# The first product of a Winograd-style MLP kernel: partial results copied into PSUM banks that later products accumulate onto

## The chip, the cores and the metric

The kernel runs on one core of one Trainium2 chip. The metric is the device time of one launch in microseconds (us); the time quoted is the median of the runs shown. Everything below refers to one profiled execution of the kernel before, with a span of 764.3 us from its first to its last instruction.

## The reference

Block-diagonal softmax attention over chunks of 64 tokens, then a gated two-layer MLP, all in fp32:

```python
scores = scale * np.matmul(q_c, k_c.transpose(0, 1, 2, 4, 3))   # 8 x 8 heads, chunks of 64, head_dim 64
attn = softmax(scores)                                          # over each chunk's 64 keys
x = np.matmul(attn, v_c)                                        # as x: (4608 tokens, 512)
h = x @ w_in                                                    # 512 -> 2048
g = h * np.clip(h + 3.0, 0.0, 6.0) / 6.0
return g @ w_out                                                # 2048 -> 512
```

## The kernel before, in words

The 4608 tokens are 9 blocks of 512. Block 0 takes the MLP in the plain way. The other eight are four pairs, 0 to 3; for each pair both matrix products are cut two by two and done with seven half-size products instead of eight (the Strassen-Winograd scheme). Every fp32 operand is split into a high and a low part, so that each 128x128x512 product is three matmuls (`passes`, L473 high by high, L474 high by low, L475 low by high); L475 alone reads the weights' low part.

**The early stage** (the first 100 us or so) loads the weights, and for each half-weight tile ScalarE makes two pieces, VectorE joins them (L215), ScalarE or VectorE takes the high part (L223, L221), and VectorE the low part (L226). For block 0 TensorE alternates the steps `a`, `b` of a tile (first product into an `h` bank, 12 matmuls in all) and `c` (12 matmuls of the second product, onto the four `acc` banks). A tile's gate is ScalarE's relu (L495), VectorE's product (L498, which frees the `h` bank), then high (L502, ScalarE) and low part (L505, VectorE). There are two `h` banks, so tile 3's `a` needs tile 1's L498 done. Between these stand the steps of the next block's attention: scores (L263), then on VectorE maximum (L275), subtraction (L279), sum (L286), reciprocal and scaling (L309) and a transposition (L335), on ScalarE the swaps that complete it (L345, five copies), on TensorE the product with v (L367).

**A pair's first product** (`first_product`, L1040) goes over 8 feature pairs p (pair 0 over 4 of them; 28 periods in all). One period is seven products of six matmuls each, named by their Winograd number in the order `ORDER_A`, and a combination on VectorE:

```python
ORDER_A = (1, 5, 6, 7, 2, 3, 4)
# p1 = copy of 1 (ScalarE, L1090); u2 = 6 + p1; u4 = 5 + u2; s7 = 7 + u4; s3 = 3 + u4; s4 = 4 + u2 (VectorE, L1032)
```

Product 2 is accumulated onto bank 1, and 3 and 4 onto the banks of 5 and 7, once these have been read. So TensorE waits, within a period, for p1 ahead of 2, for u4 ahead of 3, for s7 ahead of 4. Each of the four results then has a relu (L907, ScalarE) and a gate product (L910, VectorE). Partial banks come from two rings, `h` (two banks, also used by the attention's products) and `acc` (four).

**The order of the work** on every engine is fixed before the program runs: `Schedule.order` (L102) is a list scheduler that takes each step's named predecessors, its cost and its due time, and writes one list per engine. A due time is passed back along the chain of predecessors, so changing one step's successors can move instructions anywhere in the program, on engines that the edit does not touch. On the chip every engine takes its list strictly in order.

Of the kernel before, what the change touches and what calls it, by code (L numbers as in the profile page):

```python
# [9 lines left out]
F32 = mybir.dt.float32  # L10
# [8 lines left out]
P = 128  # L19
# [14 lines left out]
PLAIN = [p + q + NFP * r for p in range(0, NPL, 2) for r in range(2) for q in range(2)]  # L34
FIRST = {0: list(range(NFT)), 1: PLAIN, 2: PLAIN}
HELD = {5: 0, 6: 4, 7: 1, 4: 5}
ORDER_A = (1, 5, 6, 7, 2, 3, 4)
ORDER_B = (1, 5, 6, 7, 2, 4, 3)
SLOTS = 7 * NFP
HALF = [slice(0, CH), slice(CH, P)]  # L40
# [109 lines left out]
def tile_kernel(ctx: ExitStack, tc: tile.TileContext, qk_in, v_in, weights, out):  # L150
# [85 lines left out]
    class Attention:  # L236
# [116 lines left out]
        def product(self, bank=None, part=(0, 1)):  # L353
            if part[0]:
                po = self.po
            elif bank:
                po = [bank().rearrange("p (a i t) -> p a i t", a=2, t=CH) for _ in HALF]
                self.src = [t.rearrange("p a i t -> p (a i) t") for t in po]
            else:
                t = self.out()  # L360
                po = self.po = [t[:, s].rearrange("p (a i t) -> p a i t", a=2, t=CH) for s in range(2)]
                self.src = t.rearrange("p s (k t) -> p s k t", t=CH)
            for a in part:
                for i in range(NB // 2):
                    for s, rows in enumerate(HALF):
                        for o in HALF:
                            PE.matmul(po[s][o, a, i, :], lhsT=self.v[rows, a, i, o], rhs=self.aT[rows, a, i, o], start=True, stop=True)  # L367

        def parts(self, x):

# [640 lines left out]
    SLOT_OF = (2, 0, 5, 6, 4, 1, 3, 7)  # L1011
    FREED = (3, 5, 7, 2, 6, 4, 1, 0)

    bank = lambda i: ps_h.tile([P, NT], F32, name="h") if i in (6, 3) else ps_o.tile([P, NT], F32, name="acc")
    take_bank = lambda i, name, until: work.take("h", 2, name, until) if i in (6, 3) else work.take("o", 4, name, until)
    fetches, shared = 0, None

    def add_fetch(s, after=()):
# [21 lines left out]
    def first_product(s):  # L1040
        work.add(f"lay{s}", "none", 0.0, [f"ul{s - 1}.{i}.{k}" for i in ORDER_B for k in range(NFP // 2)] if s else [f"out{et}" for et in range(NET)], lambda: None)
        before = f"s{s - 1}.{SLOTS - 1}" if s else f"b{2 * NFT + PLAIN[-1]}"
        g = GRAIN[s]
        ceil = lambda n: (n + g - 1) // g
        laid = {}
        for at, p in enumerate(turns(s) if s else range(NPL, NFP), 0 if s else NPL):
            t = {}
            more = lambda r, p=p: left(p + NFP * r) if s == 0 else [f"less{u}s" for u in LATER] if s == 1 and p < 2 else [f"send{u}" for u in LATER] if s == 1 and p < NPL else []
            gq = lambda r, c, p=p: gate_of(r, c, p)
            id_ = lambda name, p=p: f"{name}{s}.{p}"  # L1050
            feeds = [add_fetch(s, [f"own{NFP + p}", f"send{NFP + p}"] if s == 1 else []) for _ in range(ceil(4) + ceil(3))] if s else []
            for k, i in enumerate(ORDER_A):
                name = id_(f"f{i}.")
                j = {2: 1, 3: 5, 4: 7}.get(i, i)
                feed, until = feeds[ceil(4) * (k // 4) + k % 4 // g] if s else (None if i in (1, 2, 4) else f"less{NFP + p}s", [])
                over = s and (k % 4 % g == g - 1 or k == 6)
                after = [before, feed, f"x{s}.{i}l" if s or i in HELD else None]
                if i == j:
                    after += take_bank(i, name, [id_({1: "gate2.", 5: "gate3.", 7: "gate4.", 6: "gate7."}[i])])
                else:  # L1060
                    after.append(id_({2: "p1.", 3: "u4.", 4: "s7."}[i]))

                def product(i=i, j=j, k=k, t=t, over=over, p=p):
                    w = ahead[0][:, k % 4 % g] if s else weight_of(p, i)
                    ps = t[j] if i != j else keep_tile(t, i, lambda: bank(i))
                    for ct in range(2):
                        o = slice(ct * P, ct * P + P)
                        passes(ps, w[:, 0, o], w[:, 1, o], *operand(s, i, ct), i == j and ct == 0, ct == 1, i != j)
                    if over:
                        ahead.pop(0)  # L1070

                due = START[s] + PART * (7 * at + k)
                work.add(name, "PE", PART, after, product, due=due)
                before = name
                if over:
                    until.append(name)
                of = lambda j, t=t: lambda: t[j]

                def fresh(key, p=p):
                    if s:  # L1080
                        return (up if key == "u2" else tp).tile([P, NT], F32, name=key)
                    if p % 2 == 0:
                        laid[key] = pair_of(("p1", "u2", "u4").index(key), F32)
                    return laid[key][:, p % 2]

                new = lambda key, t=t, fresh=fresh: lambda: keep_tile(t, key, lambda: fresh(key))
                ring = "" if s else "first"
                if i == 1:
                    work.add(id_("p1."), "ACT", 0.59, [name, f"lay{s}", *work.take(ring + "p1", 2, id_("p1."), [id_("u2.")])],
                             lambda o=new("p1"), x=of(1): ACT.copy(out=o(), in_=x()), due=due)  # L1090
                elif i == 6:
                    work.add(id_("u2."), "DVE", 0.69, [name, id_("p1."), *work.take(ring + "u2", 3 if s else 2, id_("u2."), [id_("s3."), id_("s4.")])],
                             add(new("u2"), of(6), of("p1")), due=due)
                    work.add(id_("u4."), "DVE", 0.69, [id_("f5."), id_("u2."), *work.take(ring + "u4", 2, id_("u4."), [id_("s7.")])],
                             add(new("u4"), of(5), of("u2")), due=due)
                elif i == 7:
                    work.add(id_("s7."), "DVE", 0.69, [name, id_("u4.")], add(of(6), of(7), of("u4")), due=due)
                    add_relu_gate(id_("7."), id_("s7."), of(6), lambda f=gq: f(1, 1), due, more(1))
                elif i == 2:
                    add_relu_gate(id_("2."), name, of(1), lambda f=gq: f(0, 0), due, more(0))  # L1100
                elif i in (3, 4):
                    out = (lambda f=gq: f(0, 1)) if i == 3 else (lambda f=gq: f(1, 0))
                    work.add(id_(f"s{i}."), "DVE", 0.69, [name, id_("u2.")], add(of(j), of(j), of("u2")), due=due)
                    add_relu_gate(id_(f"{i}."), id_(f"s{i}."), of(j), out, due, more(int(i == 4)))
                    if i == 3 and s:
                        on = (DVE, "DVE", 0.69) if (s, p) in TDVE else (POOL, "POOL", 1.45)
                        work.add(id_("t1."), *on[1:], [id_("gate3."), id_("gate2.")], lambda f=gq, on=on[0]: on.tensor_tensor(  # L1107
                            out=f(0, 1), in0=f(0, 1), in1=f(0, 0), op=ALU.subtract))
                        work.add(id_("t2."), *on[1:], [id_("t1."), id_("gate7.")], lambda f=gq, p=p, on=on[0]: on.tensor_tensor(
                            out=t2_of(p), in0=f(1, 1), in1=f(0, 1), op=ALU.add))  # L1110
            place_at(("f", s, at), bank_h)

    def add_units(s):
# [5 lines left out]
        if s == 0:  # L1119
            for p in range(NFP):  # L1120
                gates = [f"gate{2 * NFT + p}", f"gate{NFT + p}"] if p < NPL else [f"gate3.0.{p}", f"gate2.0.{p}"]
                work.add(f"t1.0.{p}", *(("POOL", 1.45) if TPOOL else ("DVE", 0.69)), gates, lambda p=p: (POOL if TPOOL else DVE).tensor_tensor(
                    out=gate_of(0, 1, p), in0=gate_of(0, 1, p), in1=gate_of(0, 0, p), op=ALU.subtract))
                free = {0: [f"out{et}" for et in range(NET)], 1: [f"u2.0.{NFP - 1}"], 2: [f"s7.0.{NFP - 1}"], 3: [f"s3.0.{NFP - 1}", f"s4.0.{NFP - 1}"]}[p // 2]
# [172 lines left out]
```

## Time and profile before

| | |
|---|---|
| median of 3 runs | 765.55 us (765.48 to 766.66) |
| span of the profiled execution, and its instructions | 764.3 us, 13998 |
| TensorE matmul / VectorE / ScalarE / GpSimd busy | 757.2 / 640.9 / 451.2 / 69.9 us |
| share of the span | 99% / 84% / 59% / 9% |
| granted TensorE clock | 1.000 over the whole span |

The profile gives the profiled execution by its span alone; the median of the runs is 1.25 us above that, which is taken as what lies around the span. TensorE's matmuls are recorded with modelled ends, so its busy share says only that it is never long without work; waits are read from the distance between the starts of successive matmuls.

### The profile page before, as it was taken

The numbers are of one execution on the slowest core, as the hardware profiler recorded it, in microseconds if no ns is written. First come the engines' busy times: TensorE is split into PE (matmuls) and PEld (weight loads), VectorE is DVE, ScalarE is ACT, GpSimd is POOL, SyncE is SP. The second block draws the span as 40 slices with busy tenths as digits, with TensorE's granted clock in tenths as the row PEclk, the third lists the DMA queues.
The fourth block names the chain that finished last, engine by engine and source line by source line (L and its number), as shares of the span: only waits on it lengthen the run. The fifth ranks groups of instructions, "written<-read, shape, count | busy, mean of one in ns | idle before, by whom it ended". The sixth has DMA issues, their size and how long they took to land.

```text
span 764.3 us, 13998 instructions
## 1 busy us (share of the span) xinstructions
PE 757.2 (99%) x5457; PEld 621.4 (81%) x5457; DVE 640.9 (84%) x805; ACT 451.2 (59%) x884; POOL 69.9 (9%) x74
## 2 busy tenths in 40 slices
PE   8999999999999999999999999999999999999998
PEld 5788788888888888788888888888888888888887
DVE  6989989898999999898999697689996667679751
ACT  6898967675768844356884444557853333355330
POOL 0000000000000010121200103201001123221010
PEclk9999999999999999999999999999999999999999
DMA  9999999959486898986667865757657666565572
GB/s 370 406 361 374 330 354 343 314 206 313 168 288 242 294 389 279 319 267 211 216 241 243 315 229 195 256 195 274 197 195 238 218 211 193 194 207 193 193 242 90
DMA packets 67442, 198.05 MB, mean 259 GB/s; under 512 B 7024, under 2 KB 19568, under 8 KB 63024
## 3 DMA queue, kind: packets, MB, share of 16 engines
q1 hardware_dynamic: 64752, 188.90, 71.9%
q0 software_dynamic: 2480, 8.13, 2.7%
q8 instruction: 43, 0.70, 0.4%
q14 instruction: 23, 0.19, 0.1%
q10 hardware_dynamic: 144, 0.13, 0.1%
HBM read 153.09 MB, written 44.04 MB: 258 GB/s over the span
## 4 chain that ended last, share of the span: by engine, by line
PE 85%; DMA 5%; DVE 5%; ACT 3%; issue 1%; SPq 0%; DVEq 0%; ACTq 0%
PE acc L473 21%; PE acc L474 20%; PE acc L475 20%; PE h L473 7%; PE h L474 7%; PE h L475 7%; DMA wb<-w_in_out 3%; PE two L263 2%; PE h L367 1%; DMA wb<-wa 1%; DMA xd<-qk_in 1%; ACT r L212 1%; ACT e L345 1%; ACT u L208 1%; DVE u L215 1%
## 5 line engine op out<-in xcount | busy, mean ns | idle before, releaser
L473 PE MATMUL acc<-wa,ws 128*128 128x512 f32 (+1 forms) x536 | 208.8, 390 | 0.5 <-DVE u L1032 0.5
L474 PE MATMUL acc<-wa,ws 128*128 128x512 f32 (+1 forms) x536 | 207.8, 388 | 0.0
L475 PE MATMUL acc<-wa,ws 128*128 128x512 f32 (+1 forms) x536 | 207.8, 388 | 0.0
L1140 ACT CAST wa<-wb 128x1024 fp32r<-128x1024 f32 x96 | 100.1, 1053 | 78.2 <-PE acc L475 49.1
L1144 DVE TENSOR_TENSOR wa<-wb,wa 128x1024 fp32r<-128x1024 f32 x96 | 119.0, 1257 | 17.3 <-ACT wa L1140 17.2
L473 PEld LDWEIGHTS acc<-wa,ws 128*128 128x128 f32 x536 | 100.6, 188 | 22.2 <-DVE u L1032 1.3
L475 PEld LDWEIGHTS acc<-wa,ws 128*128 128x128 f32 x536 | 100.6, 188 | 20.7
L474 PEld LDWEIGHTS acc<-wa,ws 128*128 128x128 f32 x536 | 100.7, 188 | 20.2
L907 ACT ACTIVATE r<-acc,half 128x512 f32<-128x512 f32 x90 | 61.8, 688 | 35.6 <-DVE acc L1032 31.2
L907 ACT ACTIVATE r<-h,half 128x512 f32<-128x512 f32 x38 | 26.3, 692 | 86.1 <-DVE h L1032 81.4
L910 DVE SCALAR_TENSOR_TENSOR wb<-r,acc 128x512 f32<-128x512 f32 x90 | 61.1, 681 | 6.1 <-ACT r L907 6.0
L474 PE MATMUL h<-wa,ws 128*128 128x512 f32 (+1 forms) x144 | 55.2, 383 | 0.0
L475 PE MATMUL h<-wa,ws 128*128 128x512 f32 (+1 forms) x144 | 55.2, 383 | 0.0
L473 PE MATMUL h<-wa,ws 128*128 128x512 f32 (+1 forms) x144 | 55.2, 383 | 0.0
L298 ACT ACTIVATE e<-two,m 128x64 f32<-128x64 f32 x160 | 48.4, 333 | 7.8 <-DVE m L292 6.4
L1172 POOL DMA_DIRECT2D out_t<-o x15 | 8.4, 557 | 429.6 <-DVE o L1165 428.5
L1107 POOL TENSOR_TENSOR wb<-wb 128x512 f32<-128x512 f32 x18 | 25.1, 1396 | 174.7 <-DVE wb L910 142.9
L1032 DVE TENSOR_TENSOR u<-h,p 128x512 f32<-128x512 f32 x32 | 21.9, 687 | 22.8 <-PE h L475 21.9
L1032 DVE TENSOR_TENSOR acc<-acc,u 128x512 f32<-128x512 f32 x48 | 33.0, 694 | 5.8 <-PE acc L475 5.8
L298 ACT ACTIVATION_READ_ACCUMULATOR e<-two,m 128x1 f32 x160 | 36.1, 225 | 0.0
L910 DVE SCALAR_TENSOR_TENSOR wb<-r,h 128x512 f32<-128x512 f32 x38 | 25.8, 680 | 10.7 <-ACT r L907 10.7
L473 PE MATMUL acc<-wa,wa 128*128 128x512 f32 x88 | 34.6, 393 | 0.0
(247 smaller groups left out, 1460.5 us busy)
## 6 DMA issues: line engine op xcount, KB each, us to landing
ws<-b SPq DMA_DIRECT2D x84, 512.0 KB, 4.6
ws<-a SPq DMA_DIRECT2D x72, 512.0 KB, 4.6
qk<-qk_in SPq DMA_DIRECT2D x17, 1024.0 KB, 7.6
wa<-b SPq DMA_DIRECT2D x28, 512.0 KB, 5.8
v<-v_in SPq DMA_DIRECT2D x17, 512.0 KB, 5.3
wa<-w_in_out SPq DMA_DIRECT2D x8, 1024.0 KB, 12.0
wb<-w_in_out SPq DMA_DIRECT2D x8, 1024.0 KB, 11.1
a<-wa SPq DMA_DIRECT2D x32, 256.0 KB, 4.8
```

Source lines behind the costliest of these rows:

```text
L263: PE.matmul(self.s[to, a, 2 * i + k, :], lhsT=self.qk[rows, 0, 2 * i + s, o], rhs=self.qk[rows, 1, 2 * i + s, o], start=True, stop=True)
L298: ACT.activation(out=self.flat(self.e)[:, c], in_=self.flat(self.s)[:, c], func=AF.Exp, bias=self.m[:, c:c + 1], scale=SCALE, accum_out=se ...
L473: PE.matmul(ps, lhsT=a_h, rhs=b_h, start=first, stop=False, skip_group_check=more)
L474: PE.matmul(ps, lhsT=a_h, rhs=b_l, start=False, stop=False, skip_group_check=more)
L475: PE.matmul(ps, lhsT=a_l, rhs=b_h, start=False, stop=last, skip_group_check=more)
L907: ACT.activation(out=t["r"], in_=ps(), func=AF.Relu, bias=half, scale=1.0 / 6.0)
L910: work.add("gate" + name, "DVE", 0.69, ["relu" + name, *more], lambda: DVE.scalar_tensor_tensor(out=out(), in0=t["r"], scalar=1.0, in1=ps( ...
L1032: return lambda: DVE.tensor_tensor(out=out(), in0=x(), in1=y(), op=ALU.add)
L1107: work.add(id_("t1."), *on[1:], [id_("gate3."), id_("gate2.")], lambda f=gq, on=on[0]: on.tensor_tensor(out=f(0, 1), in0=f(0, 1), in1=f(0, ...
L1140: ACT.copy(out=g_ops[s, i, pp][:, :, 0], in_=src())
L1144: work.add(low, *(("POOL", 2.5) if on else ("DVE", 1.22)), [high], lambda i=i, pp=pp, src=src, on=POOL if on else DVE: on.tensor_tensor(ou ...
L1172: nc.gpsimd.dma_start(out=out[out_rows, out_cols], in_=sums_at[out_rows.start, out_cols.start])
```

## The change

In the pairs' first product three ScalarE copies take the place of three VectorE sums. Product 1's bank is copied into the bank in which product 6 will accumulate (6 then holds u2 by itself); that bank is copied into product 7's bank (7 then holds u2 + 7, and later 4 is accumulated on it); product 5 is copied to SBUF (p5) and added to 7 and to 3 on VectorE. Product 3 accumulates on 6's bank. The order becomes 1, 5, 6, 2, 7, 3, 4. Product 1 comes from the `h` ring, 5, 6 and 7 from the `acc` ring, in the second product 1, 6 and 2 from `h`. In the attention's product into separate banks only the first four matmuls start a bank. TensorE now waits for p1 ahead of 6 and of 2, for u2 ahead of 7 and of 3, for s7 ahead of 4.

```diff
-ORDER_A = (1, 5, 6, 7, 2, 3, 4)
+ORDER_A = (1, 5, 6, 2, 7, 3, 4)
...
-                            PE.matmul(po[s][o, a, i, :], lhsT=self.v[rows, a, i, o], rhs=self.aT[rows, a, i, o], start=True, stop=True)
+                            PE.matmul(po[s][o, a, i, :], lhsT=self.v[rows, a, i, o], rhs=self.aT[rows, a, i, o], start=not bank or a == i == 0, stop=True, skip_group_check=bool(bank))
...
-    bank = lambda i: ps_h.tile([P, NT], F32, name="h") if i in (6, 3) else ps_o.tile([P, NT], F32, name="acc")
+    bank = lambda i: bank_h() if i in (1, 6, 2) else bank_o()
...
+                after = [before, feed, f"x{s}.{i}l" if s or i in HELD else None, f"lay{s}" if i == 1 else id_({5: "lie.", 6: "p1.", 2: "p1.", 7: "u2.", 3: "u2.", 4: "s7."}[i])]
+                if i == 1:
+                    after += work.take("h", 2, name, [id_("gate2.")])
+                    work.add(id_("lie."), "none", 0.0, [f"lay{s}", *[x for last in ("gate7.", "gate3.") for x in work.take("o", 4, id_("lie."), [id_(last)])]],
+                             lambda t=t: t.update({j: bank_o() for j in (5, 6)}), due=due)
...
+                        passes(t[{2: 1, 3: 6, 4: 7}.get(i, i)], w[:, 0, o], w[:, 1, o], *operand(s, i, ct), fresh and ct == 0, ct == 1, not fresh)
...
                 if i == 1:
-                    work.add(id_("p1."), "ACT", 0.59, [name, f"lay{s}", *work.take(ring + "p1", 2, id_("p1."), [id_("u2.")])],
-                             lambda o=new("p1"), x=of(1): ACT.copy(out=o(), in_=x()), due=due)
+                    work.add(id_("p1."), "ACT", 0.59, [name, id_("lie.")], copy(6, 1), due=due)
+                elif i == 5:
+                    work.add(id_("p5."), "ACT", 0.59, [name, *work.take("p1" if s else "first", 2, id_("p5."), [id_("s7."), id_("s3.")])], copy("p5", 5, beside), due=due)
                 elif i == 6:
-                    work.add(id_("u2."), "DVE", 0.69, [name, id_("p1."), *work.take(ring + "u2", 3 if s else 2, id_("u2."), [id_("s3."), id_("s4.")])],
-                             add(new("u2"), of(6), of("p1")), due=due)
-                    work.add(id_("u4."), "DVE", 0.69, [id_("f5."), id_("u2."), *work.take(ring + "u4", 2, id_("u4."), [id_("s7.")])],
-                             add(new("u4"), of(5), of("u2")), due=due)
+                    work.add(id_("u2."), "ACT", 0.59, [name, *work.take("o", 4, id_("u2."), [id_("gate4.")])], copy(7, 6, bank_o), due=due)
                 elif i == 7:
-                    work.add(id_("s7."), "DVE", 0.69, [name, id_("u4.")], add(of(6), of(7), of("u4")), due=due)
+                    work.add(id_("s7."), "DVE", 0.69, [name, id_("p5.")], plus(5, 7), due=due)
...
+                elif i == 4:
+                    add_relu_gate(id_("4."), name, of(7), lambda f=gq: f(1, 0), due, more(1))
+                else:
+                    work.add(id_("s3."), "DVE", 0.69, [name, id_("p5.")], plus(6, 6), due=due)
```

The scheduler's lists move in the early stage too, well ahead of the first pair. VectorE, before, from the low part of the second half-weight tile of `w_in` (`wa1`) on; `two` is the next block's attention, `wb0` the first tile of `w_out`, `g2` the gate of tile 0, `r_510` that of tile 1:

```order
L226 TENSOR_TENSOR wa1_475<-u_418,wa1_475 128x2x512
L215 SCALAR_TENSOR_TENSOR u_479<-u_479,r_487 128x1024
L505 TENSOR_TENSOR g2_505<-r_471,g2_505 128x512
L498 SCALAR_TENSOR_TENSOR r_510<-r_510,h_447 128x512
L226 TENSOR_TENSOR wb0_519<-u_479,wb0_519 128x2x512
L215 SCALAR_TENSOR_TENSOR u_462<-u_462,r_522 128x1024
L505 TENSOR_TENSOR g0_533<-r_510,g0_533 128x512
L275 TENSOR_REDUCE m_560<-two_332 128x16
```

VectorE, now, from the same instruction on (`r_511` is tile 1's gate):

```order
L226 TENSOR_TENSOR wa1_475<-u_418,wa1_475 128x2x512
L275 TENSOR_REDUCE m_498<-two_332 128x16
L215 SCALAR_TENSOR_TENSOR u_479<-u_479,r_487 128x1024
L505 TENSOR_TENSOR g2_507<-r_471,g2_507 128x512
L279 TENSOR_TENSOR two_332<-two_332,m_498 128x1024
L226 TENSOR_TENSOR wb0_523<-u_479,wb0_523 128x2x512
L498 SCALAR_TENSOR_TENSOR r_511<-r_511,h_447 128x512
```

The attention's maximum and subtraction stand ahead of the low part of `wb0` now, and tile 1's gate product behind it. TensorE at the same place, now (`h_500` is tile 2's first product, `acc` the second product of tile 0, which before came after half of tile 3's first product):

```order
L474 MATMUL h_500<-xd_442,wa1_475 128x512
L475 MATMUL h_500<-xd_442,wa1_475 128x512
L473 MATMUL acc_539<-g2_507,wb0_523 128x512
L474 MATMUL acc_539<-g2_507,wb0_523 128x512
L475 MATMUL acc_539<-g2_507,wb0_523 128x512
L473 MATMUL acc_546<-g2_507,wb0_523 128x512
```

Tile 0's second product is six matmuls earlier in TensorE's list than before. ScalarE in pair 0's first period, now (L1087 are the copies: `acc<-h` p1, `g1<-acc` p5, `acc<-acc` u2; L345 the swaps of an attention block):

```order
L1087 COPY acc_1969<-h_1972 128x512
L1087 COPY g1_2005<-acc_1968 128x512
L345 COPY two_1698<-e_1834 128x512
L345 COPY e_1834<-e_1834 32x16x32 x2
L1087 COPY acc_2019<-acc_1969 128x512
L907 ACTIVATE r_2022<-h_1972,half_93 128x512
```

Three of the five swap copies stand between p5 and u2 here; in pair 3 the list of a period is p1, p5, u2 and the four relus, with nothing between the three copies but in its last period.

## Rows read from the trace of the kernel before

**Rows 1.** The page's first part: busy time, share of the span, instructions.

```profile
PE 757.2 (99%) x5457; PEld 621.4 (81%) x5457; DVE 640.9 (84%) x805; ACT 451.2 (59%) x884; POOL 69.9 (9%) x74
```

**Rows 2.** TensorE's own waits by releaser: us in total, times, longest.

```profile
PE acc L473 <- DVE u L1032: 0.5, 1, 0.5
...
PE two L367 <- ACT e L345: 0.3, 1, 0.3
...
PE acc L473 <- DVE g L1032: 0.2, 1, 0.2
```

**Rows 3.** Timeline of TensorE at two waits: start, duration (us), instruction, [idle before, releaser].

```profile
180.18 0.39 PE L475 MATMUL acc<-xc,wa 128*128 128x512 f32 x1
180.73 0.50 PE L473 MATMUL acc<-xd,hl 128*128 128x512 f32 x1 [0.16 <-DVE g L1032]
181.07 0.40 PE L474 MATMUL acc<-xd,hl 128*128 128x512 f32 x1
...
320.87 0.39 PE L475 MATMUL acc<-wa,ws 128*128 128x512 f32 x1
321.81 0.50 PE L473 MATMUL acc<-wa,ws 128*128 128x512 f32 x1 [0.55 <-DVE u L1032]
```

**Rows 4.** Timeline of VectorE, 24 to 38 us.

```profile
24.97 1.22 DVE L226 TENSOR_TENSOR wa<-u,wa 128x1024 fp32r<-128x1024 f32 x1
26.63 1.22 DVE L215 SCALAR_TENSOR_TENSOR u<-u,r 128x1024 int32<-128x1024 int32 x1 [0.44 <-ACT r L212]
27.77 0.68 DVE L505 TENSOR_TENSOR g<-r,g 128x512 fp32r<-128x512 f32 x1
28.37 0.68 DVE L498 SCALAR_TENSOR_TENSOR r<-r,h 128x512 f32<-128x512 f32 x1
28.97 1.23 DVE L226 TENSOR_TENSOR wb<-u,wb 128x1024 fp32r<-128x1024 f32 x1
...
31.85 1.22 DVE L275 TENSOR_REDUCE m<-two 128x16 f32<-128x1024 f32 x1
...
36.49 1.23 DVE L279 TENSOR_TENSOR two<-two,m 128x1024 f32<-128x1024 f32 x1
```

**Rows 5.** Timeline of TensorE, 25 to 34 us.

```profile
25.80 0.46 PE L263 MATMUL two<-qk 64*64 64x64 f32 x16
...
28.82 0.39 PE L475 MATMUL h<-xd,wa 128*128 128x512 f32 x1
29.11 0.50 PE L473 MATMUL h<-xa,wa 128*128 128x512 f32 x1
...
30.60 0.40 PE L473 MATMUL acc<-g,wb 128*128 128x512 f32 x1
...
33.34 0.39 PE L473 MATMUL h<-xd,wa 128*128 128x512 f32 x1
```

**Rows 6.** Timeline of ScalarE, 27 to 34 us.

```profile
27.89 1.06 ACT L223 CAST wb<-u 128x1024 fp32r<-128x1024 f32 x1 [0.19 <-DVE u L215]
...
33.15 1.14 ACT L212 ACTIVATE r<-wb 128x1024 int32<-128x1024 uint32 x1 [0.73 <-DMA wb<-w_in_out]
```

**Rows 7.** Groups of instructions by line: relu, sum onto a bank, copy p1.

```profile
L907 ACT ACTIVATE r<-acc,half 128x512 f32<-128x512 f32 x90 | 61.8, 688 | 35.6 <-DVE acc L1032 31.2 <-PE acc L475 3.5 <-DVE wb L910 0.6
...
L1032 DVE TENSOR_TENSOR acc<-acc,u 128x512 f32<-128x512 f32 x48 | 33.0, 694 | 5.8 <-PE acc L475 5.8
...
L1090 ACT COPY p<-acc 128x512 f32<-128x512 f32 x24 | 14.0, 582 | 5.8 <-PE acc L475 5.8
```

**Rows 8.** Timeline of ScalarE at an attention block's swaps.

```profile
257.66 0.59 ACT L345 COPY two<-e 128x512 f32<-128x512 f32 x1 [1.55 <-DVE e L335]
258.28 1.26 ACT L345 COPY e<-e 32x512 f32<-32x512 f32 x2
```

**Rows 9.** Timelines at pair 1's first period: product 1's last matmul, then p1 on ScalarE.

```profile
286.71 0.39 PE L475 MATMUL acc<-wa,ws 128*128 128x512 f32 x1
...
287.14 0.59 ACT L1090 COPY p<-acc 128x512 f32<-128x512 f32 x1 [0.96 <-PE acc L475]
```

More of the change, by code (lines that the diff above doesn't have):

```diff
@@ L1012, in tile_kernel @@
     FREED = (3, 5, 7, 2, 6, 4, 1, 0)
-    bank = lambda i: ps_h.tile([P, NT], F32, name="h") if i in (6, 3) else ps_o.tile([P, NT], F32, name="acc")
-    take_bank = lambda i, name, until: work.take("h", 2, name, until) if i in (6, 3) else work.take("o", 4, name, until)
+    bank = lambda i: bank_h() if i in (1, 6, 2) else bank_o()
+    take_bank = lambda i, name, until: work.take("h", 2, name, until) if i in (1, 6, 2) else work.take("o", 4, name, until)
     fetches, shared = 0, None
@@ L1053, in first_product, with product @@
                 name = id_(f"f{i}.")
-                j = {2: 1, 3: 5, 4: 7}.get(i, i)
                 feed, until = feeds[ceil(4) * (k // 4) + k % 4 // g] if s else (None if i in (1, 2, 4) else f"less{NFP + p}s", [])
                 over = s and (k % 4 % g == g - 1 or k == 6)
[L1057 to L1063, printed above, removed]
+                due = START[s] + PART * (7 * at + k)
+                after = [before, feed, f"x{s}.{i}l" if s or i in HELD else None, f"lay{s}" if i == 1 else id_({5: "lie.", 6: "p1.", 2: "p1.", 7: "u2.", 3: "u2.", 4: "s7."}[i])]
[3 more added lines that the diff above has]
+                             lambda t=t: t.update({j: bank_o() for j in (5, 6)}), due=due)
+                def product(i=i, k=k, t=t, over=over, p=p):
                     w = ahead[0][:, k % 4 % g] if s else weight_of(p, i)
-                    ps = t[j] if i != j else keep_tile(t, i, lambda: bank(i))
+                    fresh = i in (1, 5)
+                    if i == 1:
+                        t[1] = bank_h()
                     for ct in range(2):
                         o = slice(ct * P, ct * P + P)
-                        passes(ps, w[:, 0, o], w[:, 1, o], *operand(s, i, ct), i == j and ct == 0, ct == 1, i != j)
+                        passes(t[{2: 1, 3: 6, 4: 7}.get(i, i)], w[:, 0, o], w[:, 1, o], *operand(s, i, ct), fresh and ct == 0, ct == 1, not fresh)
                     if over:
                         ahead.pop(0)
-                due = START[s] + PART * (7 * at + k)
                 work.add(name, "PE", PART, after, product, due=due)
@@ L1076, in first_product @@
                     until.append(name)
-                of = lambda j, t=t: lambda: t[j]
[L1079 to L1086, printed above, removed]
@@ L1087, in first_product, with beside, copy, plus @@
-                ring = "" if s else "first"
+                def beside(p=p):
+                    if s:
+                        return tp.tile([P, NT], F32, name="p1")
+                    if p % 2 == 0:
+                        laid[0] = pair_of(1, F32)
+                    return laid[0][:, p % 2]
+                def copy(to, of, fresh=None, t=t):
+                    return lambda: ACT.copy(out=keep_tile(t, to, fresh) if fresh else t[to], in_=t[of])
+                def plus(to, of, t=t):
+                    return lambda: DVE.tensor_tensor(out=t[to], in0=t[of], in1=t["p5"], op=ALU.add)
@@ L1096, in first_product @@
                 elif i == 7:
-                    work.add(id_("s7."), "DVE", 0.69, [name, id_("u4.")], add(of(6), of(7), of("u4")), due=due)
-                    add_relu_gate(id_("7."), id_("s7."), of(6), lambda f=gq: f(1, 1), due, more(1))
+                    work.add(id_("s7."), "DVE", 0.69, [name, id_("p5.")], plus(5, 7), due=due)
+                    add_relu_gate(id_("7."), id_("s7."), of(5), lambda f=gq: f(1, 1), due, more(1))
                 elif i == 2:
                     add_relu_gate(id_("2."), name, of(1), lambda f=gq: f(0, 0), due, more(0))
[L1101 to L1104, printed above, removed]
+                elif i == 4:
+                    add_relu_gate(id_("4."), name, of(7), lambda f=gq: f(1, 0), due, more(1))
+                else:
+                    work.add(id_("s3."), "DVE", 0.69, [name, id_("p5.")], plus(6, 6), due=due)
+                    add_relu_gate(id_("3."), id_("s3."), of(6), lambda f=gq: f(0, 1), due, more(0))
@@ L1123, in add_units @@
                     out=gate_of(0, 1, p), in0=gate_of(0, 1, p), in1=gate_of(0, 0, p), op=ALU.subtract))
-                free = {0: [f"out{et}" for et in range(NET)], 1: [f"u2.0.{NFP - 1}"], 2: [f"s7.0.{NFP - 1}"], 3: [f"s3.0.{NFP - 1}", f"s4.0.{NFP - 1}"]}[p // 2]
+                free = {3: [f"s3.0.{NFP - 1}"]}.get(p // 2, [f"out{et}" for et in range(NET)])
                 work.add(f"t2.0.{p}", *(("POOL", 1.45) if TPOOL else ("DVE", 0.69)), [f"t1.0.{p}", f"gate{2 * NFT + NFP + p}" if p < NPL else f"gate7.0.{p}", *free], lambda p=p: (POOL if TPOOL else DVE).tensor_tensor(
```

## The prediction, made before the changed kernel ran

> **What bounds the kernel now.** I read the busy shares first: TensorE is busy for 757.2 of 764.3 us, VectorE for 640.9, ScalarE for 451.2 [rows 1]. That share says only that TensorE is never long idle, so next I looked for its waits, since only a wait of TensorE can be won back. After the first 20 us, which the change leaves as they are, the wait list has three [rows 2]: 0.5 and 0.2 us on a VectorE sum, both in a pair's first product, and 0.3 us on the attention's swaps at 81 us. The true price is read from starts. In full flow a matmul starts every 0.228 us: 12 of them take from 30.60 to 33.34 [rows 5]. At 180.18 the next two starts take 0.89 us in place of 0.46, so 0.43 us is lost. At 320.87 the next start takes 0.94, and the one behind a wait takes 0.34 [rows 3], so 0.82 is lost. The wait at 81 us costs 0.28 plus the same 0.11 of restart, 0.4. All that could be won is 0.43 + 0.82 + 0.4, or 1.6 us: 0.2% of the time, about what a measurement of this kernel can tell from no change (1.53 us). The 16% of idle time on VectorE and what it is freed of are worth nothing beyond these waits.
>
> **The change, part by part.** *Sums and copies.* In 28 periods VectorE loses three sums of 0.69 us each (58 us), ScalarE gains two copies of 0.58 (33 us) [rows 7]. Neither is time of TensorE. The PSUM-to-PSUM copy is not in the trace; the nearest rows are p1 out of PSUM (0.58) and the swap into PSUM (0.59) [rows 7, 8]. I take 0.58, and up to 0.8 would still be hidden below. The number of matmuls is the same, so their time is.
>
> *The old waits.* u4 no longer exists, so the waits of 0.43 and 0.82 us go: 1.25 us. What is late next is in the following item.
>
> *New waits with one product of cover.* Product 6 follows p1 with only product 5 (6 x 0.228 = 1.37 us) between, 7 follows u2 with only 2, and 4 follows s7 with only 3. p1 starts 0.43 us after the start of product 1's last matmul (286.71 to 287.14) [rows 9], ends at 1.01, and a release costs 0.06 (VectorE's gate product ends at 29.05, TensorE starts at 29.11) [rows 4, 5]. Product 6 is due at 7 x 0.228 = 1.60, so 0.5 us is spare; for s7, at 0.69 us, 0.4. What is queued ahead decides. The longest honest chain is relu 2, gate 2, s7: relu 0.43 to 1.12, gate to 1.86, s7 to 2.5, release 2.6, against product 4's due time at 13 x 0.228 = 2.96: 0.3 to 0.4 is left. So an undisturbed period costs nothing. Where ScalarE has one instruction of 0.6 to 1.1 us between two copies it still fits, as the copies are 1.37 us or more apart. I went through the 28 periods in the new lists and found one that does not fit: pair 0's first, where the swaps stand between p5 and u2. p5 starts at 0.43, the swaps take 0.59 and 1.26 [rows 8], so u2 starts near 2.8 and is through at 3.4, product 7 is due at 2.96: 0.5 us lost. For the rest I take 0.2 us in all, between 0 and 1. Behind u2 stand relu 2 and the later swaps, so they slip by as much, but the attention's product stands in front of product 4 there and covers it.
>
> *The early stage.* This is where the lists moved most, with no edit there. VectorE's list now has the attention's maximum right behind the low part of wa1. The scores end at 26.26 [rows 5], VectorE is free at 26.19 [rows 4], so the maximum starts at about 26.3. A 1024-column instruction holds VectorE for 1.14 us (26.63 to 27.77), a 512-column one for 0.60 [rows 4]. So: join 27.5, low part of tile 0's gate 28.6, subtraction 29.2, low part of wb0 30.35, and its 1.23 us end at 31.6. Before, it started at 28.97 and ended at 30.20 [rows 4]. The high part on ScalarE follows the join by 1.06 us [rows 6] and is not the late one. TensorE meets it sooner: tile 0's second product now comes right behind tile 2's first product, whose last matmul starts at 28.82 [rows 5]. Its third matmul (L475) needs the low part; it would start at 28.82 + 3 x 0.228 = 29.5, and now starts at 31.6 + 0.06. With the restart, 2.1 + 0.1 = 2.2 us. Before, tile 3 lost 0.06 waiting for its bank, and 0.11 of restart, at 29.11 [rows 5], so the net loss is 2.1 us. Tile 3's first product, which needs VectorE's gate product behind wb0 (free at 32.2), comes at 34.0 and waits for nothing.
>
> Carrying the same addition down VectorE's list, with ScalarE held at 33.15 by the load of wb1 as before [rows 6], the low part of wa2 comes at 40.0 and tile 2's gate at 42.9, each 0.3 to 0.4 us after TensorE wants it. I take 0.6 us for the two, between 0 and 1.2, since eight instructions are added up. From there TensorE is some 2.7 us later than before, and VectorE and ScalarE are not, so the wait of 0.4 us at 81 us goes.
>
> *Moved banks, queues and order.* In the second product the banks of 1, 2 and 3 change rings; a product there is 48 matmuls, 10.9 us, and each bank's last reader is a copy or sum near the start of such a stretch. I cost it at nothing; without that cover a late VectorE sum would cost about its own 0.7 us. SP's list moves a few loads and stores past one another; the loads that TensorE stood close to (wa2, wb1, wa3) keep their places. GpSimd's list keeps its kinds and order.
>
> **The sum:** 2.1 + 0.6 - 0.4 - 1.25 + 0.5 + 0.2 = +1.75 us on 764.3, say 766.1. The median shown stands 1.25 above the profiled span, so **767.3 us**. With the bounds of the early follow-ups and of the tight waits (0 to 1.2, 0 to 1) this case alone reaches from 766.2 to 768.9.
>
> **The rivals.**
>
> *The early loss is smaller and the gains hold* (the other side). Mechanism: VectorE reaches the maximum only if the scores' last piece is there; if the scheduler's list lets TensorE run on, or VectorE does the subtraction in the shadow of a later load, the low part of wb0 is late by 1 us instead of 2.1, and tiles 2 and 3 repay the rest, as VectorE has 0.44 us idle ahead of the join [rows 4]. The swap's 0.5 us goes as well if the flip comes before p5. Price: 1.0 - 1.6 = -0.6, or 764.9 us; it decides at an early loss below 1.6 us. For it: the three waits are real and do go. Against: both lists are strictly in order, and the low part is five instructions down. Should the early loss be nil, 764.0, the most that can be gained.
>
> *A repeating gap.* If something of 0.2 us that I don't see (a slower copy between banks, a late release) sits on the relu-gate-s7 chain, it is paid in every period: 28 x 0.2 = 5.6 us, 772.9. It decides where a period's spare 0.3 us is gone. For it: three waits per period have half the cover they had. Against: every link has its duration in a row. The Trainium skill speaks for this one (Perfetto Trace Analysis, Identifying the Most-Contended Engine): the same gap repeating on the engine that should be saturated can mean too little PSUM for the next tile. By it the change, which holds three accumulating banks per period instead of releasing sums to SBUF, would show such gaps. The trace before has no repeating gap, two waits in 28 periods, so I give it little.
>
> *The change does nothing that counts.* Lists and waits end where they were: 765.5.
>
> **How the numbers follow.** The forecast 0.70, of which two thirds lie over the 0.2% line (767.08): 0.47 slower, 0.23 same. The smaller early loss 0.17: 0.12 same, 0.05 faster. The repeating gap 0.10, slower. Nothing that counts 0.03, same. Faster 0.05, same 0.38, slower 0.57. The range leaves out the repeating gap and the best half of the smaller loss: from 765.2, and above to 769.8, the forecast's own upper end and one more wait of a microsecond.
>
> **What would show it.** Right: a gap of about 2 us in TensorE near 29.5, released by VectorE's L226 on wb0; tile 3's first product at about 34.0 where TensorE had finished the same work at 32; no wait of TensorE on VectorE near 320; one wait of half a microsecond on a ScalarE copy in pair 0's first period; VectorE's busy time down by 58 us and ScalarE's up by 33. Wrong: TensorE runs through 29 to 32 us; or a gap at every seventh product.

## The result, and the profile of the changed kernel

The changed kernel takes 773.97 us (median of 4 runs, 773.76 to 774.18), the kernel before in the same comparison 765.76: a ratio of 1.0107 (95% interval 1.0094 to 1.012), 8.2 us slower. The forecast was 767.3 us with a range up to 769.8: the sign was right, the size was not. Of the profiled execution (span 772.4 against 764.3) the first part of the page and TensorE's wait list (releaser, us in total, times, longest):

```profile
PE 759.8 (98%) x5457; PEld 622.3 (81%) x5457; DVE 588.6 (76%) x721; ACT 484.2 (63%) x940; POOL 70.5 (9%) x74
```

```profile
PE acc L475 <- issue: 3.7, 1, 3.7
PE acc L475 <- DVE wb L226: 1.1, 1, 1.1
...
PE acc L473 <- DVE acc L1090: 0.7, 1, 0.7
PE acc L473 <- ACT wb L223: 0.6, 1, 0.6
...
PE acc L473 <- ACT acc L1087: 0.2, 1, 0.2
```

VectorE has 52 us less to do (58 were forecast; of two sums back to back the next starts 0.60 us after the last, so that 0.09 of each 0.69 overlaps) and ScalarE 33 more [rows 1], and the wait list has grown from three entries of the pairs and the attention [rows 2] to five. Its longest has no releaser at all: "issue" means that the engine waited for nothing that the profile shows.

The early stage is the one that was forecast. VectorE, 25 to 33 us:

```profile
25.07 1.22 DVE L226 TENSOR_TENSOR wa<-u,wa 128x1024 fp32r<-128x1024 f32 x1
26.44 1.22 DVE L275 TENSOR_REDUCE m<-two 128x16 f32<-128x1024 f32 x1 [0.15 <-PE two L263]
27.59 1.22 DVE L215 SCALAR_TENSOR_TENSOR u<-u,r 128x1024 int32<-128x1024 int32 x1
...
29.32 1.23 DVE L279 TENSOR_TENSOR two<-two,m 128x1024 f32<-128x1024 f32 x1
30.45 1.22 DVE L226 TENSOR_TENSOR wb<-u,wb 128x1024 fp32r<-128x1024 f32 x1
```

and TensorE, 28 to 33 us:

```profile
28.94 0.39 PE L475 MATMUL h<-xd,wa 128*128 128x512 f32 x1
29.93 0.50 PE L473 MATMUL acc<-g,wb 128*128 128x512 f32 x1 [0.61 <-ACT wb L223]
30.27 0.40 PE L474 MATMUL acc<-g,wb 128*128 128x512 f32 x1
31.72 0.50 PE L475 MATMUL acc<-g,wb 128*128 128x512 f32 x1 [1.06 <-DVE wb L226]
```

and ScalarE's high part:

```profile
28.84 1.05 ACT L223 CAST wb<-u 128x1024 fp32r<-128x1024 f32 x1
```

The maximum and the subtraction stand ahead of the low part of `wb0`, which starts at 30.45 and not at 28.97 [rows 4]; TensorE restarts at 31.72 (forecast 31.66). The high part on ScalarE was late too (it ends at 29.89, where TensorE could have gone on at 29.17), so the loss is in two pieces.

What was not forecast is at 269 us, in pair 0's second product. TensorE there:

```profile
267.87 1.11 PE L263 MATMUL two<-qk 64*64 64x64 f32 x64
268.91 0.50 PE L473 MATMUL acc<-wa,wa 128*128 128x512 f32 x1
269.25 0.40 PE L474 MATMUL acc<-wa,wa 128*128 128x512 f32 x1
273.34 0.50 PE L475 MATMUL acc<-wa,wa 128*128 128x512 f32 x1 [3.69 <-issue]
273.68 0.48 PE L473 MATMUL acc<-wa,wa 128*128 128x512 f32 x1
273.96 0.63 PE L474 MATMUL acc<-wa,wa 128*128 128x512 f32 x1
```

and the same stretch by windows (us, busy time and count by engine, granted clock, DMA share, GB/s):

```profile
265.00:270.00 5.00, 4.65 (x139) 3.55 (x137) 5.00 (x5) 3.58 (x5) 0.66 (x2) 1.00 0.93 283
270.00:275.00 5.00, 1.66 (x5) 1.33 (x6) 2.09 (x4) 0.00 (x0) 0.00 (x0) 0.88 0.83 329
275.00:280.00 5.00, 5.00 (x19) 4.04 (x18) 1.40 (x2) 2.00 (x2) 0.00 (x0) 0.77 0.29 83
```

The third of three matmuls on one bank, with all its data at hand, starts 4.09 us after the second (0.23 in full flow). Behind the pause the granted clock is below 1: TensorE runs at the lower of its levels, 1.2 GHz, with starts 0.427 apart, and comes back to 2.4 GHz near 277. The pause costs 3.86 us, the restart behind it 0.11 and the slow stretch 1.61: 5.6 us.

The wait at 320 us has stayed. VectorE and TensorE:

```profile
315.39 1.23 DVE L309 TENSOR_TENSOR two<-two,z 128x1024 f32<-128x1024 f32 x1
319.34 0.69 DVE L586 TENSOR_TENSOR wb<-wb 128x512 f32<-128x512 f32 x1 [2.72 <-DMA wb<-wa]
...
321.00 0.69 DVE L1090 TENSOR_TENSOR acc<-acc,p 128x512 f32<-128x512 f32 x1
```

```profile
320.63 0.39 PE L475 MATMUL acc<-wa,ws 128*128 128x512 f32 x1
321.75 0.50 PE L473 MATMUL acc<-wa,ws 128*128 128x512 f32 x1 [0.73 <-DVE acc L1090]
```

VectorE stands 2.72 us at the fold (L586, a sum on a reloaded weight tile) for a transfer issued at 313.26; s7 (321.00) is queued behind it, and TensorE loses 1.0 us. In the kernel of before VectorE stood at the same fold, for a transfer issued at 305.34:

```profile
310.58 0.70 DVE L1032 TENSOR_TENSOR h<-acc,u 128x512 f32<-128x512 f32 x1
313.09 0.69 DVE L586 TENSOR_TENSOR wb<-wb 128x512 f32<-128x512 f32 x1 [1.81 <-DMA wb<-wa]
...
321.06 0.69 DVE L1032 TENSOR_TENSOR u<-acc,u 128x512 f32<-128x512 f32 x1
```

There s7 of the same period (310.58) stood ahead of the fold, and what came late was the next period's u4 (321.06), for which TensorE lost 0.82 [rows 3]. Now the list has the fold ahead of s7, and VectorE, with fewer sums in front, comes to it 3.4 us after the transfer's issue and not 5.9.

Times by the same rule as in the prediction (distance of starts less 0.227), changed kernel less kernel before: early gap 2.22 - 0.17; at 40 and 43 us 0.28 + 0.31; 81 us 0.09 - 0.44; pair 0's first period 0.49; 180 us -0.43; 269 us 5.58; 320 us 1.00 - 0.82. The sum is 8.1, as between the spans.

### The profile page after: what moved, and what is told of

Same layout as the page of the kernel before. It is cut to its first block, busy times and chain, and to the rows that moved or that the text cites. A ratio compares the mean times of both kernels' runs of the same rounds, so it can differ in the third digit from the quotient of the medians.

```text
span 772.4 us, 13982 instructions
## 1 busy us (share of the span) xinstructions
PE 759.8 (98%) x5457; PEld 622.3 (81%) x5457; DVE 588.6 (76%) x721; ACT 484.2 (63%) x940; POOL 70.5 (9%) x74
## 4 chain that ended last, share of the span: by engine, by line
PE 94%; DMA 3%; ACT 1%; DVE 1%; issue 1%; SPq 0%; DVEq 0%
PE acc L473 18%; PE acc L475 18%; PE acc L474 18%; PE h L473 12%; PE h L475 12%; PE h L474 12%; PE two L263 2%; PE h L367 2%; DMA wa<-w_in_out 2%; DMA wb<-wa 1%; DMA qk<-qk_in 1%; PE two L367 0%; PE acc L367 0%; PE h L488 0%; ACT r L212 0%
## 5 line engine op out<-in xcount | busy, mean ns | idle before, releaser
L473 PE MATMUL acc<-wa,ws 128*128 128x512 f32 (+1 forms) x432 | 168.2, 389 | 0.7 <-DVE acc L1090 0.7
L475 PE MATMUL acc<-wa,ws 128*128 128x512 f32 (+1 forms) x432 | 167.3, 387 | 0.0
L474 PE MATMUL acc<-wa,ws 128*128 128x512 f32 (+1 forms) x432 | 167.3, 387 | 0.0
L475 PE MATMUL h<-wa,ws 128*128 128x512 f32 (+1 forms) x248 | 95.6, 386 | 0.0
L473 PE MATMUL h<-wa,ws 128*128 128x512 f32 (+1 forms) x248 | 95.6, 386 | 0.0
L474 PE MATMUL h<-wa,ws 128*128 128x512 f32 (+1 forms) x248 | 95.6, 386 | 0.0
L473 PEld LDWEIGHTS acc<-wa,ws 128*128 128x128 f32 x432 | 81.1, 188 | 18.0 <-DVE acc L1090 1.2
L475 PEld LDWEIGHTS acc<-wa,ws 128*128 128x128 f32 x432 | 81.1, 188 | 16.6
L474 PEld LDWEIGHTS acc<-wa,ws 128*128 128x128 f32 x432 | 81.1, 188 | 16.3
L907 ACT ACTIVATE r<-acc,half 128x512 f32<-128x512 f32 x90 | 60.1, 689 | 43.1 <-DVE acc L1090 33.1
L474 PEld LDWEIGHTS h<-wa,ws 128*128 128x128 f32 x248 | 46.6, 188 | 9.4
L473 PEld LDWEIGHTS h<-wa,ws 128*128 128x128 f32 x248 | 46.6, 188 | 9.4
L475 PEld LDWEIGHTS h<-wa,ws 128*128 128x128 f32 x248 | 46.6, 188 | 9.3
L1090 DVE TENSOR_TENSOR acc<-acc,p 128x512 f32<-128x512 f32 x48 | 33.5, 697 | 17.7 <-PE acc L475 12.2
```

The costliest lines, as they stand in the source:

```text
L473: PE.matmul(ps, lhsT=a_h, rhs=b_h, start=first, stop=False, skip_group_check=more)
L474: PE.matmul(ps, lhsT=a_h, rhs=b_l, start=False, stop=False, skip_group_check=more)
L475: PE.matmul(ps, lhsT=a_l, rhs=b_h, start=False, stop=last, skip_group_check=more)
L907: ACT.activation(out=t["r"], in_=ps(), func=AF.Relu, bias=half, scale=1.0 / 6.0)
L1090: return lambda: DVE.tensor_tensor(out=t[to], in0=t[of], in1=t["p5"], op=ALU.add)
```

## The experiments

**Is the pause at 269 us a wait for instructions?** The trace has a DMA queue of kind "instruction" with 43 packets of 16384 bytes in a run; TensorE's 11,125 recorded instructions, shared out, are 259 for each, and the last five packets start 259, 271, 243 and 254 of them apart. Two views of the changed kernel's transfers, from 252.9 to 271.05 us and from there to 271.3 (queue, packets, MB, share):

```profile
q1 hardware_dynamic: 1382, 5.00, 82.4%
q0 software_dynamic: 266, 0.90, 12.2%
...
wa<-b SPq DMA_DIRECT2D x6, 512.0 KB, 8.0
...
q1 hardware_dynamic: 22, 0.05, 50.0%
q0 software_dynamic: 13, 0.04, 36.7%
q8 instruction: 1, 0.02, 23.9%
```

None comes for 18 us, then one, in the middle of the pause (271.09 to 272.04). Theory: a packet is a block of TensorE's instructions, the attention block (64 + 64 short matmuls, 256 instructions with the weight loads) eats one in 2 us, and the next comes too late for that. The first variant moves where blocks end:

```diff
     warm_up(WARM)
+    few = ps_h.tile([P, NT], F32, name="h")
+    for _ in range(20):
+        PE.matmul(few[:, :CH], lhsT=nought.broadcast_to([P, P]), rhs=nought.broadcast_to([P, CH]), start=True, stop=True)
```

> Changed kernel plus 20 short matmuls (64 columns, 40 instructions with their weight loads) ahead of the first load, where TensorE waits for data: nothing of the order, the data or the transfers of pair 0 is touched, only the number of instructions that TensorE has read by a given step. Theory (instructions): the 4.09 us at 269.25 are a wait for TensorE's next block of instructions, because a block ends right where the attention block's 256 short instructions begin, which then eat the next one in 2 us. Shifted by 40 instructions the block is asked for some 4.5 us earlier, so the stall and the slow clock behind it go: 774.0 - 5.6 = 768.4 us, and the other waits (30, 169.5, 320 us) stay. Rival (transfers): TensorE is held by the burst of transfers at 262 to 271 us whatever it reads then; the stall stays, 774.0 us.

Measured: 773.08 us (770.5 to 774.49; ratio to before 1.009, interval 1.0076 to 1.0104). The median did not fall to 768.4, but the pause at 269 us is gone, and another of the same kind stands at 20 us, in a first attention block, with the slow clock behind it. TensorE there:

```profile
19.91 0.55 PE L469 MATMUL s<-xc,g 64*64 64x64 f32 x24
22.35 0.34 PE L469 MATMUL s<-xc,g 64*64 64x64 f32 x8 [1.90 <-issue]
```

Counted in the records, TensorE had taken 4801 instructions at the pause of the changed kernel and 704 at this one: 18 x 256 + 193 and 2 x 256 + 192. 17 packets had come before the first and one before the second, so both pauses stand where the packets so far are used up (448 + 17 x 256 = 4800, 448 + 256 = 704). The position theory holds; the place for the extra instructions was badly chosen. They were put past the loading stage next, beside the changed kernel itself as a control on the same chip:

```diff
                     if i == 1:
                         t[1] = bank_h()
+                        for _ in range(20 if (s, p) == (0, NPL) else 0):
+                            PE.matmul(t[1][:, :CH], lhsT=nought.broadcast_to([P, P]), rhs=nought.broadcast_to([P, CH]), start=True, stop=True)
```

> The changed kernel again, as the control on the same chip as the three others, since the variants before spread over 4 us from run to run where the kernel of before spreads over 1. Theory: its extra time is made of waits for transfers (the block of instructions at 269 us, 3.4 to 5.7 us with the slow clock; a weight tile's reload at 320 us, 1.0 to 1.9 us), whose length goes with the traffic, so it spreads from 770 to 774 us too, with a median near 773. Rival (the spread belongs to the variants): 773.8 to 774.2 us, as first measured.

> Changed kernel plus 20 short matmuls (40 instructions, about 0.5 us) into product 1's bank ahead of pair 0's first product, past the loading stage. Theory: all stalls seen without a releaser fell behind instruction 192 of a block of 256 (4800 = 18 x 256 + 192, and 704 = 2 x 256 + 192 in the variant with the short matmuls at the start); here the block ends 40 instructions, 4.5 us, earlier than the attention block begins, so the stall at 269 us and the slow clock go: control - 3.4 to 5.7 + 0.5, some 768.5 to 770.5 us, with the waits at 30, 169.5 and 320 us still there. Rival (traffic alone): control + 0.5.

Measured: control 773.97 us (772.43 to 775.09; 1.0103, 1.0089 to 1.0117), with the short matmuls 770.26 (769.89 to 771.8; 1.0059, 1.0046 to 1.0071). 3.7 us go, although the short matmuls cost 0.65, and TensorE's wait list from 100 us on has no "issue" left:

```profile
PE acc L473 <- DVE acc L1092: 1.0, 1, 1.0
PE acc L473 <- ACT acc L1089: 0.2, 1, 0.2
```

Nothing of the data, the order or the transfers of pair 0 was touched: what TensorE lacked at 269 us was its next block of instructions. The control also shows what varies from run to run in the changed kernel. In its profiled execution the pause at 269 us costs 0.9 us only, and the one behind the fold 2.45, with the slow clock after that one:

```profile
318.39 0.50 PE L473 MATMUL acc<-wa,ws 128*128 128x512 f32 x1 [2.18 <-DVE acc L1090]
```

**Is it the change's doing, or the place of a block's end?** The kernel of before, with 14 short matmuls at the same place, so that its attention block at 262 us begins where a block of instructions does:

```diff
                     ps = t[j] if i != j else keep_tile(t, i, lambda: bank(i))
+                    for _ in range(14 if (s, p, i) == (0, NPL, 1) else 0):
+                        PE.matmul(ps[:, :CH], lhsT=nought.broadcast_to([P, P]), rhs=nought.broadcast_to([P, CH]), start=True, stop=True)
```

> Kernel of before plus 14 short matmuls (28 instructions, about 0.35 us) at the same place, which moves the attention block at 262 us from 29 instructions ahead of the end of a block of instructions to 1. Theory (position makes the stall; traffic sets its length): TensorE stalls after the attention block there too, by the packet's delay of 1.1 us as in the kernel of before + 0.96 for the packet + 1.3 from its end to the restart - 2.3 us in which the block is used up = 1.0 us, up to 3 if the traffic is worse: 767 to 769 us, against 765.9. Rival (the changed kernel's transfers make the stall): 766.2 us, no stall.

Measured: 767.45 us (766.46 to 769.85; ratio 1.0022, 1.0013 to 1.0031). The kernel of before gets the pause, 1.1 us between starts (0.15 at this place without one), at the same instruction 4800:

```profile
263.06 1.11 PE L263 MATMUL two<-qk 64*64 64x64 f32 x64
265.07 0.50 PE L473 MATMUL acc<-wa,wa 128*128 128x512 f32 x1 [0.90 <-issue]
```

So it needs none of the changed arithmetic. The change put its attention block 25 instructions further down TensorE's list (from 4515 to 4540) and so onto a block's end (4544).

**What sets its length?** The two stores of pair 0 that GpSimd issues at 264.6 us, left out:

```diff
-                if n == 1:
+                if n == 1 and not (s == 0 and out_rows.start < 2 * P and not fresh):
                     nc.gpsimd.dma_start(...)
```

> Changed kernel without the two stores (0.5 MB) of pair 0's product-2 sums that GpSimd issues at 264.6 us; that part of the output is left unwritten. Theory (instructions behind a burst): the block of instructions came late because its packet stood behind 1.5 MB issued between 262.4 and 265.8 us; without a third of them it comes about 1.3 us earlier, and the stall at 269.25 shrinks from 3.9 us to 2.5 or less, 771 to 772.6 us; if the stores alone delayed it, the stall goes and 768.4 us are left. Rival (position alone: the block is late because 256 instructions are read in 2 us, whatever is being transferred): no change, 774.0 us.

Measured: 772.5 us (770.39 to 774.66; 1.0087, 1.0072 to 1.0101); the pause is 3.45 us between starts in its profile, against 4.09. That is in the direction of the theory, but in the two profiles of the changed kernel itself, with nothing taken out, the pause costs 0.9 and 4.0 us: inconclusive. In all six profiles in which the attention block sits there unshifted, and in the kernel of before with 14 matmuls, the packet ends 1.3 to 1.6 us ahead of the restart, so the pause follows the packet; what delays the packet stays open.

**The early stage alone.** Five due times of the planner set back to what they were, which restores the engines' lists up to 140 us:

```diff
             latest[n] = min([self.due[n]] + [latest[m] - self.steps[m][1] - SETTLE for m in then[n]])
+            latest[n] = {"a42": 104.62, "a43": 107.47, "b43": 108.89, "own9": 107.92, "top12": 109.03}.get(n, latest[n])
```

> Changed kernel with five due times of the planner (latest of a42, a43, b43, own9, top12) set to what they were before the change, which gives every engine its old list up to 140 us. Theory (my forecast's early item): the two gaps at 28.9 to 31.7 us and those at 40 and 43 us go, the old wait of 0.4 us at 81 us comes back: 2.45 us less, 771.5 us if the stall at 269 us stays as it is. The number of instructions ahead of pair 0 is the same but all transfers are earlier by 2.5 us with TensorE, so the stall should stay within a microsecond or two; if it goes too, 766.0 us. Rival (the early gaps are absorbed later by some other wait): 774.0 us.

Measured: 771.98 us (770.11 to 774.43; 1.0078, 1.0064 to 1.0092), 2 us under the changed kernel, which was not run on the same chip; what went is read from the trace. The gaps at 30, 40 and 43 us are gone and 0.46 at 81 us is back. But TensorE, 2.5 us earlier at pair 0, now waits there five times for 0.2 to 0.8 us, 2.0 us in all: a part of the gain is given back.

**Has a period spare time?** The copy of product 1 made twice, in all 28 periods:

```diff
-... [name, id_("lie.")], copy(6, 1), due=due)
+... [name, id_("lie.")], lambda f=copy(6, 1): (f(), f()), due=due)
```

> Changed kernel in which ScalarE makes the copy of product 1 twice, in all 28 periods (0.58 us more on ScalarE ahead of product 6). Theory (forecast's spare of 0.5 us, from starts 0.43 us behind the last matmul, 0.58 for the copy and 0.06 for the release against 1.60): the second copy ends 0.05 to 0.1 us after product 6 is due, so each period pays 0.1 to 0.2 us with the restart: 28 x 0.15 = 4 us, 778 us, between 775 and 781. Rival 1 (the copies have no spare left, each period is on the edge): 28 x 0.7 = 19 us, 793 us. Rival 2 (the spare is larger than I worked out, or the second copy overlaps the first): 774.0 us.

Measured: 779.57 us (775.83 to 780.88; 1.0171, 1.0152 to 1.019). ScalarE and TensorE in pair 1's first period:

```profile
294.57 1.17 ACT L1087 COPY acc<-h 128x512 f32<-128x512 f32 x2 [2.06 <-PE h L475]
```

```profile
295.51 0.39 PE L475 MATMUL acc<-wa,ws 128*128 128x512 f32 x1
295.80 0.50 PE L473 MATMUL acc<-wa,ws 128*128 128x512 f32 x1
296.13 0.39 PE L474 MATMUL acc<-wa,ws 128*128 128x512 f32 x1
```

The two copies end at 295.74, product 6 starts at 295.80 in place of 295.74, and with the restart (0.34 in place of 0.23) the period loses 0.17 us. It repeats in all 28 periods, twice that in three of them. 0.06 us over the edge with 0.57 added: the spare was 0.5 us, as worked out.

**The wait at 320 us.** The fold one period later, in the changed kernel and (behind s4 of period 6) in the kernel of before:

```diff
-        work.add(f"comb{u}", "DVE", 0.67, [f"whole{u}"], lambda f=combine: f(0))
+        work.add(f"comb{u}", "DVE", 0.67, [f"whole{u}", "s7.1.7" if u == 11 else None], lambda f=combine: f(0))
```

> Changed kernel in which VectorE's fold of the last streamed weight tile (unit 11) is put one period later, behind product 7's sum of period 7. Theory: at 316.6 us VectorE stands 2.7 us at the head of its list for the tile's reload (6 us after its issue), and s7 is queued behind it; with s7 ahead TensorE's 1.0 us (1.9 in two variants) at 320 us goes: control - 1.0 to - 1.9 us. Rival (the wait moves on with the fold, or the due time moves the lists elsewhere): control within 0.5 us.

> Kernel of before with the fold of unit 11 some five instructions later in VectorE's list, behind s4 of period 6. Theory: the wait of 0.82 us at 320.9 us came from the 1.81 us that VectorE stood at the fold's reload two periods earlier; it goes, 766.0 - 0.8 = 765.2 us, a little below both kernels. Rival (the fold's 1.2 us low part now stands between u2 and u4 of the next period and makes TensorE wait there): 766.0 to 766.5 us.

Measured: changed kernel 771.92 us (770.26 to 773.06; 1.0082, 1.0068 to 1.0096), 2.05 under the control (the intervals of the two ratios overlap), and no wait of TensorE between 312 and 334 us; kernel of before 765.46 (764.99 to 765.78; 0.9993, 0.9985 to 1.0002), its 0.82 at 321 us down to 0.14. Both waits came from a transfer at the head of VectorE's list and from what stood behind it there, not from the sum that TensorE waited for. The second kernel is the lowest of the study, but its interval holds 1.

**Do the losses add?** The short matmuls and the later fold, together with u2's copy ahead of the swaps in pair 0's first period, and together with the five due times:

```diff
-            before = work.add(name + u, engine, cost, [before, *more], f, due=due)
+            before = work.add(name + u, engine, cost, [before, *more, "u2.0.4" if name + u == "down30" else None], f, due=due)
```

> Changed kernel with three of its losses taken out at once: the 20 short matmuls ahead of pair 0 (against the stall at 269 us), the fold of unit 11 one period later (against the wait at 320 us), and in pair 0's first period u2's copy ahead of the second swap of the attention block instead of behind it. Theory: each is a loss of its own, so they add: 770.3 (with the short matmuls alone) - 1.1 to 1.9 - 0.5 = 768.4 us, between 767.9 and 768.9; what is left above 766.0 is the early stage (2.5 us) less the old waits, and 0.5 us of short matmuls. Rival (the waits hide one another, so that the next one in line comes up): 769.5 us or more.

> Changed kernel with the short matmuls, the later fold of unit 11 and the old due times of the early stage. Theory from the run with the early due times alone: the 2.45 us of the early stage are won, 0.45 at 81 us come back, and some 2 us of them are given back in pair 0, where TensorE is early and VectorE isn't (waits at 164, 173, 187 and 193 us): 770.3 - 1.1 - 2.45 + 0.45 + 2.1 = 769.3 us, between 768 and 770. Rival (those pair 0 waits were chance): 767.2 us.

Measured: 770.45 us (769.38 to 772.13; 1.0063, 1.005 to 1.0077) and 767.53 us (766.91 to 768.79; 1.0026, 1.0015 to 1.0037). The first missed. The waits at 169.5 and 320 us are gone, and two new ones stand in pair 0, on u2's and on p1's copy:

```profile
183.48 0.50 PE L473 MATMUL acc<-wa,hl 128*128 128x512 f32 x1 [0.76 <-ACT acc L1089]
191.19 0.50 PE L473 MATMUL acc<-wa,hl 128*128 128x512 f32 x1 [0.59 <-ACT acc L1089]
```

ScalarE, ahead of the first of them:

```profile
182.24 0.32 ACT L298 ACTIVATE e<-two,m 128x64 f32<-128x64 f32 x1 [1.65 <-DVE m L292]
...
182.83 0.59 ACT L1089 COPY acc<-acc 128x512 f32<-128x512 f32 x1
```

The one predecessor added moved the exponentials of the next attention block ahead of u2, and they wait for a VectorE step (L292) that is itself behind a fold. The second did better than I expected, since pair 0's waits are 1.6 us there and not the 2.1 that I took. Its 767.53 less 0.65 for the short matmuls is 766.9: rid of its three accidents, the changed kernel is still about 1 us above the kernel of before.

## Why the prediction was right and wrong

*The early stage* (2.1 + 0.6 us): right, 2.05 + 0.59, at the place and down the list that were given; the run with the old due times shows the list as the cause. The low part of `wb0` sets its end, as forecast. But "the high part on ScalarE ... is not the late one" was a misreading: its 1.06 us are its own length [rows 6] and begin at the join's end, so that by the forecast's own times it ends near 29.8, and it made the first 0.9 us of the gap. The low part hid that. *81 us* (-0.4), *pair 0's first period* (0.5) and *180 us* (-0.43): right, -0.35, 0.49 and -0.43. *The tight new waits* (0.2, between 0 and 1): nothing was lost in the other 27 periods; the spare of 0.5 us was shown by doubling the copy. The copy between banks took 0.57 us, where 0.58 was taken.

*The old waits* ("u4 no longer exists, so the waits of 0.43 and 0.82 us go"): wrong for the second. I took the releaser that the wait list names, a sum, and did not ask what that sum had stood behind: 1.81 us at a transfer, 7.8 us earlier. The sum is gone, the transfer is not; VectorE comes to it sooner and waits longer, the new list has s7 behind it, and s7 inherits the wait: 1.00 for 0.82, where I had 0. That is 1.0 us of the miss.

*Moved banks, queues and order* ("I cost it at nothing"): wrong, and this is the other 5.6 us. I followed each list for data and banks and took TensorE's own list as free to run wherever its data are there. It has a supply of its own: blocks of 256 instructions, of which it had, in these runs, no more than one ahead. 24 matmuls of 512 columns take 5.4 us for 48 instructions; an attention block takes 256 in 2 us. Where a block of instructions ends just as an attention block begins, and the packet of the next but one ends 1.7 to 5.2 us after that (DMA share 0.93 from 265 to 270 us), TensorE stands. 25 instructions decided it. The Trainium skill (Runtime: NRT & Kernel Launch, Instruction fetch mechanics) says that instructions come in blocks of 16 KiB, 256 instructions, and that crossing a block's end is "mostly hidden". The packets agree with the block's size. The second holds for nearly all of the 43 packets of a run, which come without a pause; it does not at the 1.0 to 4.1 us of the runs here, where short matmuls follow one another while the queues are busy.

With the two items put right the sum is 1.75 + 5.6 + 1.0 = 8.35, less 0.2 that was taken for waits which cost nothing: 8.15, against 8.1 between the spans. Two slips of the forecast count for less: the 1.25 us added to the span are nearer 1.8 (774.18 against 772.4 in one execution), and its bounds give 766.5 to 768.7, not 766.2 to 768.9. *The repeating gap*, which I gave 0.10 and whose 772.9 us lies near the result, is not what happened: no gap repeats from period to period, and that the one-off losses sum to about as much is chance. The Trainium skill has the sentence on repeating gaps in Perfetto Trace Analysis, Optimization Strategy. *The smaller early loss* is refuted by the 2.1 us.

My range held the bounds of every cost that I had named and had no room for one that I hadn't. Nothing that I read for this forecast counted TensorE's instructions, so the stall could not be forecast from those rows; a list that moved by 25 instructions with no edit there should have been worth more than "nothing".

## What to carry to other kernels

Where a wait is to be won back, follow its releaser up its own list until something that is no computation: if that is a transfer, making the releaser cheaper lets it wait longer. A gap without a releaser on TensorE, behind many short matmuls, is to be held against the count of its instructions (here all fell at 191 to 193 past a multiple of 256; a few instructions are missing from the records); a few extra instructions ahead of it tell in one run. And where a planner hands due times back along chains, an edit in one stage has its price where the lists moved: read these first.

## What the runs showed of the hardware that was not expected

- TensorE pauses where a block of 256 of its instructions ends, if the next block's 16 KB packet is late: 1.0 to 4.1 us between starts in eight profiles, the packet ending 1.3 to 1.6 us ahead of the restart in all of them.
- After four of these pauses, after one wait of 2.2 us on VectorE (the control) and once after the early gaps (the first variant), the granted clock fell to 1.2 GHz for about eight matmuls (starts 0.427 us apart), at a cost of some 1.6 us each time; after the other four pauses it did not. The length of the pause does not decide it here: behind 2.75 us between starts (the copy made twice) the clock fell, behind 2.73 (the old due times) it stayed.
- The changed kernel, whose two longest waits are for transfers, spread from 772.4 to 775.1 us on one chip, where the kernel of before stayed within 765.4 to 766.3; on the chip of the first comparison its four runs lay within 0.4 us, so the spread is not always there.
